# Products with v in groups of three key chunks, with a fourth exponential tile

## The chip, the cores and the metric

The kernel runs on one core of a Trainium2 chip. The metric is the device time of one execution in microseconds (us). The engines of the core are named as in the profile: PE is TensorE's matmul, PEld its weight load, DVE is VectorE, ACT is ScalarE, POOL is GpSimd and SP is SyncE, whose queue issues most DMAs.

## What is computed

One input x of 2048 tokens by 576 features goes through two branches, whose outputs are mixed by a gate per token:

```python
B, S, D = 1, 2048, 576
H = 32; Dh = D // H                    # 32 heads of 18
qkv = (x @ wqkv).reshape(B, S, 3, H, Dh)
scores = einsum("bhqd,bhkd->bhqk", q, k) * Dh ** -0.5
a = (softmax(scores) @ v) @ wo
h = gelu(layernorm(x) @ w1 + b1)       # 576 to 4608
b = h @ w2 + b2                        # 4608 to 576
g = sigmoid((x * gate_w).sum(-1))
out = g * a + (1 - g) * b
```

All of it is float32. The kernel keeps that precision with fp32r matmuls by splitting operands into a high and a low part and adding three products.

## The kernel before

**Attention.** The 32 heads form 16 pairs, and each pair is worked on in two halves of 1024 query tokens: 32 units. A unit has 16 chunks of 128 keys, so the main loop has 512 *steps* (`NSTEP`). In a step, `s2` (L268) is called twice, for two blocks of 512 queries. Each call makes the scores of both heads with two matmuls (L279), one in rows 0 to 63 of the array and one in rows 64 to 127, and ACT takes their exponentials into a tile of `RING` (L281). Between the two matmuls of `s2` stands a *round* of the maxima: two matmuls of the transposed scores (L204) whose maxima DVE reduces (L206). The rounds run about 20 steps ahead of the scores, since a unit's maxima enter its scores as two extra rows of q. They end at step 492.

**Products with v.** `pv` (L296) multiplies exponentials with v (L308): for a key chunk eight records, in four column tiles of 32, into one PSUM bank that sums a unit's 16 chunks. It is called in every even step for the two chunks before it. `RING` has three tiles: two from the pool `pp`, used at first for staging weights, and `ring2`. When a unit's sum is complete, `o_store` (L315) copies the bank with DVE and sends it off. The PSUM has three banks for the maxima (`ps_s1`), one for the sums (`ps_o`), two for scores and two for the MLP.

**MLP.** It runs in the gaps of the attention, as a generator that yields after each slot of two matmuls. It takes four token blocks, and for each nine groups of four chunks of the 4608 hidden features. A group has two *up pairs* (`h_pair`, L523: two chunks of hidden features, 27 slots that the planner counts at 231 ns, L547) and four *out pairs* (`out_pair`, L643: 128 tokens, 24 slots of 131 ns, L679). The order is up, four outs of the group before, up, so that two up pairs stand next to each other; in a block's last group the second up pair stands between the second and the third out pair. An up pair is followed by the gelu in pieces: ACT adds the bias (L572) and squares (L635), POOL multiplies (all POOL operations have line L160), ACT takes the Tanh (L628), and POOL multiplies again, rounds to `hh` and subtracts to `hl`, the two parts that the out pairs use. In the first token block the weights are split too: ACT copies (L444), POOL subtracts, and the parts go to scratch in HBM, from where the other blocks load them.

**The planner.** The order of every engine's queue is fixed when the program is built. `run_due` (L135) is called once per `s2`, per group of products and per piece of MLP; it advances a slot count and a clock `now` by the planned time, and issues what has come due: operations set for a slot (`defer`), those set for a time (`queue_end`, from `pool_end`, the planned end of POOL's work), and background work on POOL such as the split of w1, which may start when `pool_end` is less than 950 ns ahead of `now`.

**The gaps.** A step has two places, one behind each `s2`. In every two steps one place holds `pv` and three hold a *piece* of MLP, which `fill` (L1301) takes by running the generator to its next cut. Where an up pair is cut follows from `piece`, the place's number: in three pieces, or in six where the MLP is ahead of its target (`behind`) or the pair is the first of a group. An out pair is cut in three. The work is paced so that 32.6 us of MLP by the planner's count (`KEPT`) remain when the maxima end. Between two `s2` calls with nothing between them, the second waits for a bank until the exponential has read it.

**Loads of k and v.** `KA` has three tiles, taken in turn by the pairs. k, q and v of later pairs are loaded in the second step of a unit, on SP's queue.

Of the kernel before, what the change touches and what calls it, by code (L numbers as in the profile page):

```python
# [17 lines left out]
P = 128  # L18
# [36 lines left out]
BARE = NSTEP - LEAD - NT  # L55
KEPT = (FIN - BARE) / 2 * 4650.0


@with_exitstack
def gated_mix_kernel(ctx: ExitStack, tc: tile.TileContext, x, wqkv, wo, w1, b1, w2, b2, gate_w, out):  # L60
# [33 lines left out]
    ps_s1 = ctx.enter_context(tc.tile_pool(name="ps_s1", bufs=NS1, space=PSUM))  # L94
    ps_o = ctx.enter_context(tc.tile_pool(name="ps_o", bufs=1, space=PSUM))
    QA = [att.tile([P, HALF], F32R, name=f"qa{i}") for i in range(3)]
    KA = [att.tile([P, S], F32R, name=f"ka{i}") for i in range(3)]
# [81 lines left out]

    def load_k(pair, c0=0, c1=S):  # L180
        ka = KA[pair % 3]
# [11 lines left out]
    def s1_round(u, r):  # L193
# [5 lines left out]
        qa, ka = QA[u % 3], KA[UNITS[u][0] % 3]  # L199
# [38 lines left out]
    RING = []  # L238
    ybusy = [0]
# [28 lines left out]
    def s2(u, kc, qb, around, ns):  # L268

        flush()  # L270
        qa, ka = QA[u % 3], KA[UNITS[u][0] % 3]
# [4 lines left out]
        def head(h):  # L276
            ps = psum(ps_s2)
            r0 = 64 * h
            nc.tensor.matmul(ps, ka[r0:r0 + 56, kc * P:(kc + 1) * P], qa[r0:r0 + 56, qb * TB:(qb + 1) * TB],  # L279
                             start=True, stop=True)  # L280
            nc.scalar.activation(RING[n % 3][:, qb, h], ps, AF.Exp, scale=SCALE)  # L281

# [13 lines left out]
    def pv(n):  # L296

        flush()
        u, kc = divmod(n, NT)
        if kc == 0:  # L300
            OB[u] = psum(ps_o)
        v = VT[UNITS[u][0] % 2]
        for c in (n, n + 1):
            for qb in range(2):
                for h in range(2):
                    r = 32 * (2 * h + qb)
                    k = c % NT
                    nc.tensor.matmul(OB[u][r:r + 32, :], v[:, k, 19 * h:19 * h + 32], RING[c % 3][:, qb, h, :],  # L308
                                     start=(k == 0), stop=(k == NT - 1))
        if kc == NT - 2:  # L310
            o_store(u, OB.pop(u))
# [62 lines left out]
    def mlp():  # L374
# [148 lines left out]
        def h_pair(q, last, inner=False):  # L523
# [16 lines left out]
            ends = cuts(27, (5, 5, 4)[piece[0]] if last else (3, 5, 4)[piece[0]])  # L540
            if (last or spent[0] > behind[0] + AHEAD) and piece[0] == 0 and not late:

                ends = {4, 9, 14, 18, 23}
# [99 lines left out]
        def out_pair(i, t, acc):  # L643
# [12 lines left out]
            ends = {7, 15} if piece[0] == 0 else cuts(24, (3, 2, 1)[piece[0]])  # L656
# [120 lines left out]
    piece = [0]  # L777
    behind = [0.0]
# [41 lines left out]
    with ExitStack() as a:  # L820
# [205 lines left out]
        for i in range(3):  # L1026
# [82 lines left out]

    RING.append(ring2)  # L1110

# [4 lines left out]
    def out_proj():  # L1116
# [49 lines left out]
        def load_o(b, first=True, last=True):  # L1166

            if first:
                o = x_tile().rearrange("p (c n) -> p c n", c=5)
                ka, qa = {0: (KA[1], QA[2]), 1: (KA[1], QA[2]), 2: (KA[2], QA[0]), 3: (KA[1], QA[2])}[b]  # L1170
# [130 lines left out]
    def fill(step, share):  # L1301

        gap = 3 * (step // 2) + share
        t = spent[0]
        if over[0] is None and rounds:
            piece[0] = share
            behind[0] = base + (TOTAL - KEPT - base) * step / BARE
            atom()
            run_due(max(spent[0] - t, GAP))
        elif over[0] is None:  # L1310
            if not bare_at:
                bare_at.extend((gap, spent[0]))
            g0, s0 = bare_at
            stretch(s0 + (TOTAL - s0) * (gap + 1 - g0) / (1.5 * FIN - g0) - spent[0])
# [9 lines left out]
    looped[0] = True  # L1324
    for u in range(NU):
        for kc in range(NT):
            step = u * NT + kc
            if kc == 1:
                if u + 2 < NU:
                    load_q(u + 2)  # L1330
                if u % 2 == 0 and u // 2 + 1 < NPAIR - 1:
                    load_k(u // 2 + 1)
                    load_v(u // 2 + 1)
                elif u == NU - 5:
                    load_k(NPAIR - 1)
                elif u == NU - 4:
                    load_v(NPAIR - 1)
            at[0] = step

            s2(u, kc, 0, loop_round(), 462.0)  # L1340
            if kc % 2:
                fill(step, 1)
            elif step > 0:
                pv(step - 2)
                run_due(2080.0)
                if step <= 2 * LEAD:
                    next_round()
            else:
                fill(step, 2)
            s2(u, kc, 1, loop_round(), 462.0)  # L1350
            fill(step, 2 if kc % 2 else 0)
    pv(NSTEP - 2)
# [28 lines left out]
```

## Time and profile before

| | |
|---|---|
| median of 3 runs | 2254.62 us (2254.19 to 2256.15) |
| the profiled execution | 2255.1 us |
| its span | 2253.3 us |
| mean clock granted to TensorE | 0.998 |
| instructions | 51099 |
| DMA | 323.61 MB, 144 GB/s over the span |

The profile's page lists for each engine the busy time, its share of the span and the number of instructions. A group of instructions shows line, engine, operation, output and inputs, the count, busy time, the mean duration of one in ns, and the idle time before them with what ended it. A row of the timeline shows start and duration in us, line and operation, how many are merged in the row, and in brackets the idle time before it with its releaser. A row of the list of waits shows who waited for whom, the total in us, the number of times and the longest one.

Matmuls overlap in the array, so durations of single matmuls (414 ns on average for L279) add up to more than the time that passes; the starts show the pace.

### The profile page before, as it was taken

How to read it: one execution, taken by the hardware profiler on the slowest of the kernel's cores; microseconds unless marked ns; L12 is line 12 of the kernel's file. 1: busy time of each engine (PE TensorE's matmuls, PEld its weight loads, DVE VectorE, ACT ScalarE, POOL GpSimd, SP SyncE). 2: the span in 40 equal slices, each digit the busy share in tenths (PEclk: the TensorE clock that was granted, in tenths of full speed). 3: DMA queues.
4: the chain of work that ended last, by engine and by line, in shares of the span. 5: the costliest groups of instructions: out<-in, count | busy, mean ns of one | idle time of the engine just before them, and what ended most of it. 6: DMA issues, size and time to landing. Idle time of an engine off the chain costs nothing.

```text
span 2253.3 us, 51099 instructions
## 1 busy us (share of the span) xinstructions
PE 2231.5 (99%) x20569; PEld 1649.5 (73%) x20569; DVE 1671.8 (74%) x2953; ACT 1431.6 (64%) x2623; POOL 946.2 (42%) x936
## 2 busy tenths in 40 slices
PE   8999999999999999999999999999999999999999
PEld 7878766777777777777777777777777777777769
DVE  5675877777787787778777877787778777877545
ACT  4223677777776666666666666666666666666661
POOL 4002466666664444443444344434444444444420
PEclk9999999999999999999999999999999999999999
DMA  7755655545473424243264424243465233323355
GB/s 244 261 189 184 193 164 164 173 131 163 133 223 137 149 98 126 98 128 108 89 177 153 120 97 131 90 122 120 122 167 159 98 120 115 106 99 115 109 177 193
DMA packets 163218, 323.61 MB, mean 144 GB/s; under 512 B 59646, under 2 KB 86178, under 8 KB 152146
## 3 DMA queue, kind: packets, MB, share of 16 engines
q1 hardware_dynamic: 158982, 313.57, 44.0%
q10 hardware_dynamic: 4000, 6.78, 0.8%
q8 instruction: 162, 2.65, 0.5%
q14 instruction: 74, 0.61, 0.1%
HBM read 229.07 MB, written 95.16 MB: 144 GB/s over the span
## 4 chain that ended last, share of the span: by engine, by line
PE 92%; POOL 3%; DVE 2%; ACT 2%; DMA 1%; issue 0%; SPq 0%; ACTq 0%; DVEq 0%; POOLq 0%
PE ps L308 20%; PE ps L679 19%; PE ps L547 18%; PE ps L279 14%; PE ps L204 11%; PE ps L955 4%; PE ps L1263 3%; PE ps L973 2%; POOL zz L160 1%; POOL hl L160 1%; POOL w L160 1%; DVE m L206 1%; PE ps L870 0%; DMA p<-in_A_wqkv_dram 0%; ACT p L281 0%
## 5 line engine op out<-in xcount | busy, mean ns | idle before, releaser
L206 DVE TENSOR_REDUCE m<-ps 128x1 f32<-128x512 f32 x2048 | 1301.1, 684 | 299.6 <-PE ps L204 254.4
L281 ACT ACTIVATE p<-ps 128x512 f32<-128x512 f32 x1368 | 743.5, 596 | 377.5 <-PE ps L204 231.3
L279 PE MATMUL ps<-qa,ka 56*128 56x512 f32 x2048 | 715.1, 414 | 4.8 <-ACT p L281 3.8
L204 PE MATMUL ps<-ka,qa 54*128 54x512 f32 x2048 | 647.2, 418 | 3.8 <-DVE m L206 2.6
L679 PE MATMUL ps<-w,hh 64*128 64x288 f32 x4352 | 526.2, 296 | 2.4 <-ACT z L572 1.6
L279 PEld LDWEIGHTS ps<-qa,ka 56*128 56x128 f32 x2048 | 359.8, 185 | 229.6 <-issue 113.5
L547 PE MATMUL ps<-big,w 64*128 64x512 f32 x3888 | 513.9, 390 | 0.2 <-ACT vt L984 0.2
L160 POOL TENSOR_SCALAR zz<-zz 128x512 f32<-128x512 f32 x272 | 168.8, 621 | 776.5 <-ACT zz L635 693.9
L281 ACT ACTIVATE ring<-ps 128x512 f32<-128x512 f32 x680 | 369.6, 596 | 190.4 <-PE ps L204 124.9
L547 PEld LDWEIGHTS ps<-big,w 64*128 64x128 f32 x3888 | 401.6, 185 | 51.9 <-ACT vt L984 0.4
L679 PEld LDWEIGHTS ps<-w,hh 64*128 64x128 f32 x4352 | 421.7, 186 | 15.9 <-ACT z L572 2.1
L160 POOL TENSOR_TENSOR zz<-zz,z 128x512 f32<-128x512 f32 x280 | 361.4, 1291 | 34.5 <-ACT zz L637 10.5
L679 PE MATMUL ps<-w,hl 64*128 64x288 f32 x2176 | 364.8, 292 | 0.0
L204 PEld LDWEIGHTS ps<-ka,qa 54*128 54x128 f32 x2048 | 333.5, 185 | 30.0 <-DVE m L206 10.4
L308 PE MATMUL ps<-p,vt 128*32 128x512 f32 x2736 | 344.5, 598 | 0.0
L679 PEld LDWEIGHTS ps<-w,hl 64*128 64x128 f32 x2176 | 246.4, 185 | 1.4
L160 POOL TENSOR_TENSOR w<-x,w 128x576 fp32r<-128x576 f32 (+1 forms) x34 | 69.0, 2033 | 295.7 <-ACT w L444 276.5
L308 PEld LDWEIGHTS ps<-p,vt 128*32 128x32 f32 x2736 | 71.4, 109 | 153.9 <-issue 147.9
L308 PE MATMUL ps<-ring,vt 128*32 128x512 f32 x1360 | 179.1, 598 | 0.0
L160 POOL TENSOR_TENSOR hl<-zz,hh 128x512 fp32r<-128x512 f32 x134 | 172.5, 1287 | 15.2 <-ACT hh L598 4.3
L653 DVE SCALAR_TENSOR_TENSOR x<-ps,x 128x288 f32<-128x288 f32 x270 | 110.8, 452 | 83.3 <-PE ps L679 80.9
L955 PE MATMUL ps<-big,wqk 128*128 128x512 f32 x504 | 121.5, 396 | 0.4 <-ACT wqk L863 0.4
(118 smaller groups left out, 1382.8 us busy)
## 6 DMA issues: line engine op xcount, KB each, us to landing
w<-w_scr SPq DMA_DIRECT2D x54, 1152.0 KB
w<-w_scr SPq DMA_DIRECT2D x108, 576.0 KB
w_scr<-w SPq DMA_DIRECT2D x18, 1152.0 KB
w_scr<-w SPq DMA_DIRECT2D x36, 576.0 KB
qa<-qk_scr SPq DMA_DIRECT2D x192, 72.0 KB
ka<-qk_scr SPq DMA_DIRECT2D x90, 144.0 KB
x<-in_B_w_dram SPq DMA_DIRECT2D x34, 288.0 KB
qk_scr<-hh SPq DMA_DIRECT2D x36, 256.0 KB
```

Source lines behind the costliest of these rows:

```text
L160: fn(*args, **kw)
L204: nc.tensor.matmul(ps, qa[r0:r0 + 54, t * P:(t + 1) * P], ka[r0:r0 + 54, kb * TB:(kb + 1) * TB], start=True, stop=True)
L206: nc.vector.tensor_reduce(M4[u][:, h, t, kb:kb + 1], ps, axis=AX.X, op=ALU.max)
L279: nc.tensor.matmul(ps, ka[r0:r0 + 56, kc * P:(kc + 1) * P], qa[r0:r0 + 56, qb * TB:(qb + 1) * TB], start=True, stop=True)
L281: nc.scalar.activation(RING[n % 3][:, qb, h], ps, AF.Exp, scale=SCALE)
L308: nc.tensor.matmul(OB[u][r:r + 32, :], v[:, k, 19 * h:19 * h + 32], RING[c % 3][:, qb, h, :], start=(k == 0), stop=(k == NT - 1))
L547: nc.tensor.matmul(ps[h], wt[w_][r, c, :], Y[s_][r, c, :], start=(k == 0), stop=(k == 26))
L653: nc.vector.scalar_tensor_tensor(dst, ps[nn][:, :ND], 0.5, b2b[:, cs[nn]] if base else dst, op0=ALU.mult, op1=ALU.add)
L679: mm = nc.tensor.matmul(ps[nn][:, :ND], h_[r, tok], w_[p_][r, cs[nn]], start=(k == 0 or bare and k == 3 * G), stop=(k == 6 * G - 1 or bare ...
L955: nc.tensor.matmul(ps, w_[:, c, ms], big[:, s_, :], start=(k == 0), stop=(k == len(prods) - 1))
L973: nc.tensor.matmul(ps[:, :ND], big[:, s_, tok], w_[:, c, cs], start=(k == 0), stop=False)
L1263: nc.tensor.matmul(ps[t, n][:, :ND], OT[b][3][:, s_, tok], w_part(w_, c)[:, cs], start=(c == 0 and k == 0), stop=(c == 4 and k == 1))
```

## The change

A fourth tile joins `RING`. It takes the place of the third tile of `KA` (8 KB per partition each), and the third tile of `KA` comes back in its place at step 433, for the last pair alone. As long as four tiles are there (up to step 428), `pv` is called with all chunks in waiting when three wait, or when a pair of the MLP has ended and at least one waits. It may now reach from one unit into the next, so the bank of the sums is taken from a rotation that it shares with the maxima: a new sum takes the bank that is next in turn, and the old sum's bank goes to the end of the turn. `piece` counts the places since the last products, and with three chunks in waiting an up pair is cut in five pieces if it begins behind them. From step 428 on, products take two chunks again and the old cuts hold. The load of v for a later pair waits until the products that still read the tile are issued.

```diff
+NARROW = 431
...
-    ps_s1 = ctx.enter_context(tc.tile_pool(name="ps_s1", bufs=NS1, space=PSUM))
-    ps_o = ctx.enter_context(tc.tile_pool(name="ps_o", bufs=1, space=PSUM))
+    ps_x = [ctx.enter_context(tc.tile_pool(name=f"ps_x{i}", bufs=1, space=PSUM)) for i in range(NS1 + 1)]
+    turn_x = list(range(NS1))
+    held_x = [NS1]
+    class Rotating:
+        def tile(self, *args, **kw):
+            i = turn_x.pop(0)
+            turn_x.append(i)
+            return ps_x[i].tile(*args, **kw)
+    class Sums:
+        def tile(self, *args, **kw):
+            i = turn_x.pop(0)
+            turn_x.append(held_x[0])
+            held_x[0] = i
+            return ps_x[i].tile(*args, **kw)
+    ps_s1 = Rotating()
+    ps_o = Sums()
...
-    KA = [att.tile([P, S], F32R, name=f"ka{i}") for i in range(3)]
+    KA = [att.tile([P, S], F32R, name=f"ka{i}") for i in range(2)]
...
+    def k_tile(pair):
+        return KA[2 if pair == NPAIR - 1 else pair % 2]
...
+    def ring(n):
+        return RING[n % 4 if n < NARROW else (n - NARROW) % 3]
...
-    def pv(n):
+    def pv(n0, n1):
         flush()
-        u, kc = divmod(n, NT)
-        if kc == 0:
-            OB[u] = psum(ps_o)
-        v = VT[UNITS[u][0] % 2]
-        for c in (n, n + 1):
+        for c in range(n0, n1):
+            u, k = divmod(c, NT)
+            if k == 0:
+                OB[u] = psum(ps_o)
+            v = VT[UNITS[u][0] % 2]
             for qb in range(2):
                 for h in range(2):
...
-        if kc == NT - 2:
-            o_store(u, OB.pop(u))
+            if k == NT - 1:
+                o_store(u, OB.pop(u))
+        run_due(1040.0 * (n1 - n0))
...
-            ends = cuts(27, (5, 5, 4)[piece[0]] if last else (3, 5, 4)[piece[0]])
-            if (last or spent[0] > behind[0] + AHEAD) and piece[0] == 0 and not late:
-                ends = {4, 9, 14, 18, 23}
+            if room[0] == 3:
+                ends = cuts(27, max(1, 5 - piece[0]))
+            else:
+                ends = cuts(27, (5, 5, 4)[piece[0]] if last else (3, 5, 4)[piece[0]])
+                if (last or spent[0] > behind[0] + AHEAD) and piece[0] == 0 and not late:
+                    ends = {4, 9, 14, 18, 23}
...
-            ends = {7, 15} if piece[0] == 0 else cuts(24, (3, 2, 1)[piece[0]])
+            ends = {7, 15} if piece[0] == 0 else cuts(24, max(1, 3 - piece[0]))
...
-        for i in range(3):
+        for i in range(2):
             for j in range(2):
                 nc.gpsimd.memset(KA[i][64 * j + 32:64 * j + 64, :].bitcast(F32), 1.0)
...
+    ring_stack = ExitStack()
+    RING.append(ring_stack.enter_context(tc.tile_pool(name="c_ring", bufs=1, side="right")).tile([P, 2, 2, TB], F32, name="ring3"))
...
-    def fill(step, share):
-        gap = 3 * (step // 2) + share
+    ended = [0]
+    def fill(step):
         t = spent[0]
+        gap = gaps[0]
+        gaps[0] += 1
         if over[0] is None and rounds:
-            piece[0] = share
             behind[0] = base + (TOTAL - KEPT - base) * step / BARE
-            atom()
+            ended[0] = atom() == 2
+            piece[0] += 1
             run_due(max(spent[0] - t, GAP))
...
                 if u % 2 == 0 and u // 2 + 1 < NPAIR - 1:
                     load_k(u // 2 + 1)
-                    load_v(u // 2 + 1)
+                    due_v.append((u * NT, u // 2 + 1))
                 elif u == NU - 5:
+                    ring_stack.close()
+                    kp = ctx.enter_context(tc.tile_pool(name="c_ka", bufs=1, side="right"))
+                    KA.append(kp.tile([P, S], F32R, name="ka2"))
+                    for j in range(2):
+                        nc.gpsimd.memset(KA[2][64 * j + 32:64 * j + 64, :].bitcast(F32), 1.0)
                     load_k(NPAIR - 1)
                 elif u == NU - 4:
-                    load_v(NPAIR - 1)
+                    due_v.append((u * NT, NPAIR - 1))
             at[0] = step
+            room[0] = 3 if step < NARROW - 3 else 2
+            while due_v and due_v[0][0] <= done[0]:
+                load_v(due_v.pop(0)[1])
             s2(u, kc, 0, loop_round(), 462.0)
-            if kc % 2:
-                fill(step, 1)
-            elif step > 0:
-                pv(step - 2)
-                run_due(2080.0)
-                if step <= 2 * LEAD:
+            if step - done[0] >= room[0] or room[0] == 3 and ended[0] and step > done[0]:
+                pv(done[0], step)
+                done[0] = step
+                piece[0] = 0
+                ended[0] = 0
+                if extra[0]:
                     next_round()
+                    extra[0] -= 1
             else:
-                fill(step, 2)
+                fill(step)
             s2(u, kc, 1, loop_round(), 462.0)
-            fill(step, 2 if kc % 2 else 0)
-    pv(NSTEP - 2)
+            if not (room[0] == 3 and ended[0]):
+                fill(step)
+    pv(done[0], NSTEP)
```

More of the change, by code (lines that the diff above doesn't have):

```diff
@@ L178, in load_q @@
                 dma_r(nc.sync, qa[r:r + DH, :], qk_scr[part, d0:d0 + DH, half * HALF:(half + 1) * HALF])
+    def k_tile(pair):
+        return KA[2 if pair == NPAIR - 1 else pair % 2]
     def load_k(pair, c0=0, c1=S):
-        ka = KA[pair % 3]
+        ka = k_tile(pair)
         for h in range(2):
@@ L198, in s1_round @@
             M4[u] = asm.tile([P, 2, 8, 4], F32, name="m4")
-        qa, ka = QA[u % 3], KA[UNITS[u][0] % 3]
+        qa, ka = QA[u % 3], k_tile(UNITS[u][0])
         def head(h):
@@ L270, in s2 @@
         flush()
-        qa, ka = QA[u % 3], KA[UNITS[u][0] % 3]
+        qa, ka = QA[u % 3], k_tile(UNITS[u][0])
         n = u * NT + kc
@@ L280, in head @@
                              start=True, stop=True)
-            nc.scalar.activation(RING[n % 3][:, qb, h], ps, AF.Exp, scale=SCALE)
+            nc.scalar.activation(ring(n)[:, qb, h], ps, AF.Exp, scale=SCALE)
         def tail():
@@ L306, in pv @@
                     r = 32 * (2 * h + qb)
-                    k = c % NT
-                    nc.tensor.matmul(OB[u][r:r + 32, :], v[:, k, 19 * h:19 * h + 32], RING[c % 3][:, qb, h, :],
+                    nc.tensor.matmul(OB[u][r:r + 32, :], v[:, k, 19 * h:19 * h + 32], ring(c)[:, qb, h, :],
                                      start=(k == 0), stop=(k == NT - 1))
-        if kc == NT - 2:
-            o_store(u, OB.pop(u))
+            if k == NT - 1:
+                o_store(u, OB.pop(u))
+        run_due(1040.0 * (n1 - n0))
     stored = []
@@ L777, in gated_mix_kernel @@
     piece = [0]
+    room = [2]
     behind = [0.0]
@@ L1169, in load_o @@
                 o = x_tile().rearrange("p (c n) -> p c n", c=5)
-                ka, qa = {0: (KA[1], QA[2]), 1: (KA[1], QA[2]), 2: (KA[2], QA[0]), 3: (KA[1], QA[2])}[b]
+                ka, qa = {0: (KA[1], QA[2]), 1: (KA[1], QA[2]), 2: (KA[0], QA[0]), 3: (KA[1], QA[2])}[b]
                 OT[b] = [o, [ka[:, c * TB:(c + 1) * TB].bitcast(F32) for c in range(4)] + [qa[:, :TB].bitcast(F32)], ka]
@@ L1311, in fill @@
             if not bare_at:
-                bare_at.extend((gap, spent[0]))
-            g0, s0 = bare_at
-            stretch(s0 + (TOTAL - s0) * (gap + 1 - g0) / (1.5 * FIN - g0) - spent[0])
+                bare_at.extend((gap, spent[0], step))
+            g0, s0, n0 = bare_at
+            stretch(s0 + (TOTAL - s0) * (gap + 1 - g0) / (1.5 * (FIN - n0)) - spent[0])
             run_due(max(spent[0] - t, GAP))
@@ L1324, in gated_mix_kernel @@
     looped[0] = True
+    done = [0]
+    due_v = []
+    extra = [LEAD]
+    gaps = [0]
     for u in range(NU):
```

## The prediction

> **What bounds the kernel now.** I read the busy shares first, then the chain of work that ended last, then what TensorE waits for, and last the timeline of TensorE around one group of products with v.
>
> ```profile
> PE 2231.5 (99%) x20569; PEld 1649.5 (73%) x20569; DVE 1671.8 (74%) x2953; ACT 1431.6 (64%) x2623; POOL 946.2 (42%) x936
> PE 92%; POOL 3%; DVE 2%; ACT 2%; DMA 1%; issue 0%; SPq 0%; ACTq 0%; DVEq 0%; POOLq 0%
> L308 PE MATMUL ps<-p,vt 128*32 128x512 f32 x2736 | 344.5, 598 | 0.0
> L308 PE MATMUL ps<-ring,vt 128*32 128x512 f32 x1360 | 179.1, 598 | 0.0
> ```
>
> TensorE is busy for 99% and makes up 92% of the chain, so what counts is how densely its matmuls stand. The products with v (L308) are 2736 + 1360 = 4096 records, eight for a key chunk: 512 chunks, and since each call of pv takes two, 256 groups. The waits of TensorE that the profile names are small:
>
> ```profile
> PE ps L870 <- DMA x<-in_A_x_dram: 6.2, 2, 5.6
> PE ps L279 <- ACT p L281: 3.8, 7, 0.6
> PE ps L204 <- DVE m L206: 2.6, 5, 0.5
> PE ps L279 <- ACT ring L281: 1.0, 2, 0.6
> ```
>
> A switch between the 64-row form of all other matmuls of the loop and the 32-column form of the products appears in no wait. It shows in start times:
>
> ```profile
> 1006.02 0.39 PE L279 MATMUL ps<-qa,ka 56*128 56x512 f32 x1
> ...
> 1006.62 1.06 PE L308 MATMUL ps<-ring,vt 128*32 128x512 f32 x8
> 1007.50 1.04 PE L308 MATMUL ps<-p,vt 128*32 128x512 f32 x8
> 1008.47 0.49 PE L279 MATMUL ps<-qa,ka 56*128 56x512 f32 x1
> ...
> 1009.04 1.09 PE L547 MATMUL ps<-big,w 64*128 64x512 f32 x8
> 1009.97 0.39 PE L279 MATMUL ps<-qa,ka 56*128 56x512 f32 x1
> ...
> 1010.43 1.38 PE L547 MATMUL ps<-big,w 64*128 64x512 f32 x10
> ```
>
> A score round (two L279, two L204) takes 1010.43 - 1009.97 = 0.46 us. From 1006.02 to 1009.04 stand two score rounds and one group: 3.02 - 0.92 = 2.10 us for the group. Its second chunk starts 0.88 us behind the first, so two chunks are 1.76 us, and **0.34 us belong to the group as such**, whatever its size. That is the change's first prize.
>
> **The count of groups.** The order of the MLP repeats after a set of two up pairs and four out pairs. Group starts in one set:
>
> ```profile
> 996.46 1.06 PE L308 MATMUL ps<-p,vt 128*32 128x512 f32 x8
> 1013.83 1.06 PE L308 MATMUL ps<-p,vt 128*32 128x512 f32 x8
> 1020.82 1.92 PE L308 MATMUL ps<-p,vt 128*32 128x512 f32 x16
> 1028.14 1.06 PE L308 MATMUL ps<-ring,vt 128*32 128x512 f32 x8
> 1050.03 1.06 PE L308 MATMUL ps<-ring,vt 128*32 128x512 f32 x8
> ```
>
> With 1006.62 above: an up pair in three pieces takes 10.16 us in two steps, one in six pieces 7.21 + 6.99 = 14.20 us in four, and the out pairs from 1020.82 to 1050.03 take 29.21 us, 7.30 each, in two steps each. That is 53.57 us, 14 steps, seven groups. Now each up pair is cut into five pieces, which fill exactly the five places that three steps leave beside one group; an out pair keeps three pieces in two steps. Again 14 steps, but six groups. The first groups still come at steps 2, 4, 6 and 8 (out pairs of three pieces). From 8 to 428, where three chunks in waiting are given up, lie 30 sets of 14 steps: 180 groups. The last 84 steps have 42. So 4 + 180 + 42 = 226, 30 fewer: 30 x 0.34 = 10.2 us. Against it stand 30 more pieces of MLP, because a place without products is filled. The up pair in six pieces over four steps takes 14.20 - 10.16 = 4.04 us more than in three over two; four score rounds and a group are 4 x 0.46 + 2.10 = 3.94, so three more cuts cost 0.10, a cut 0.03, thirty 1.0 us. **Net: -9.2 us.** By another reading of the same rows: 14.20 us less two steps without MLP, halved (4.04 / 2 = 2.02 a step), gives 14.20 - 2.02 = 12.18 for three steps at half a group each; with a third of a group, 0.17 less: 12.0 us.
>
> The page "TensorEngine Tiling (Array Packing)" of the Trainium skill, section Key Properties, says that changing the tiling mode drains the engine, and "TensorE: Matmul & The Clock Gate", section Single matmul latency, puts a drain at about 175 ns. Two drains a group would be 0.35 us, by estimate 10.5 us for thirty; the trace's 0.34 agrees.
>
> **The waits in the first quarter.** In the first token block the MLP's weights are split on ACT and POOL, and there the out pair behind two adjacent up pairs takes longer:
>
> ```profile
> 526.64 1.06 PE L308 MATMUL ps<-ring,vt 128*32 128x512 f32 x8
> ...
> 534.12 0.50 PE L279 MATMUL ps<-qa,ka 56*128 56x512 f32 x1 [0.58 <-ACT ring L281]
> ...
> 535.03 1.06 PE L308 MATMUL ps<-p,vt 128*32 128x512 f32 x8
> ```
> ```profile
> 532.95 0.63 ACT L628 ACTIVATE zz<-zz 128x512 f32<-128x512 f32 x1 [1.43 <-POOL zz L160]
> 533.49 1.07 ACT L281 ACTIVATE ring<-ps 128x512 f32<-128x512 f32 x2
> ```
> ```profile
> 520.07 2.69 POOL L160 TENSOR_TENSOR w<-x,w 128x1152 fp32r<-128x1152 f32 x1 [1.58 <-ACT w L444]
> ```
>
> 8.39 us in place of 7.30: a Tanh (L628) stands 1.43 us in ACT's queue for POOL, the exponentials behind it come late, and TensorE's next scores wait for their banks. Of the nine waits for L281 in the list above, seven lie in seven such sets: 7 x 1.09 = 7.6 us. POOL is late because the split at 520.07 lies between the multiplies of the first up pair. The planner lets this split out only while pool_end is under 950 ahead of now. Count from the products before the first up pair: four splits of w2 (1555 each by pool_op) bring pool_end to 8761 from the first place at 2541; at the last fill now is 7623, 1138 ahead: not yet, and the square and the first multiplies come before it. With five pieces the first place is at 1848, pool_end 8068, and at the score round before the last fill now is 7392: 676 ahead, so the split goes out **before** the first up pair ends. I therefore expect most of this wait to go. But the split's copy then falls between exponentials, and the second up pair is 2.2 us shorter, so POOL has less time: bounds are all 7.6 us gained and, with the split still late, 11 us lost (per set the 1.43 us once more, now for hl; 0.61 us for two score rounds with no piece between, two exponentials of 1.07 less 0.46; as much again where the split's copy stands ahead of exponentials; less the 1.09). I take -4, nearer to the gain because the planner's sums put the split early.
>
> **Later blocks** split nothing. POOL's work for one up pair there:
>
> ```profile
> 1008.55 0.62 POOL L160 TENSOR_SCALAR zz<-zz 128x512 f32<-128x512 f32 x1 [27.36 <-ACT zz L635]
> ...
> 1010.63 0.62 POOL L160 TENSOR_SCALAR zz<-zz 128x512 f32<-128x512 f32 x1
> ...
> 1019.41 1.30 POOL L160 TENSOR_TENSOR hl<-zz,hh 128x512 fp32r<-128x512 f32 x1
> 1022.73 0.62 POOL L160 TENSOR_SCALAR zz<-zz 128x512 f32<-128x512 f32 x1 [2.03 <-ACT zz L635]
> ```
>
> 12.2 us from 1008.55 to 1020.71, then 2.03 idle. Twelve microseconds an up pair use this idle time up but need no more. Here it starts 1.93 us behind the products' start at 1006.62; products of three chunks last 0.34 + 3 x 0.88 = 2.98, so then it starts 1.05 before their end. The second up pair's first multiplies (2.1, from 1008.55 to 1010.63) are done at -1.05 + 12.2 + 2.1 = 13.2 us behind that end, and their Tanh has its turn on ACT at about 14.9: three steps, 12.0, a score round, 0.46, a piece of seven slots at the planner's 131 ns, 0.92, another round, and its two exponentials, 1.09. 1.7 us remain: I cost it at nothing, and at 1.09 us a set if that cover is gone (second rival).
>
> **The last part.** From 428 groups take two chunks again and up pairs ahead of their target six pieces, 16 steps a set. 9 up and 20 out pairs remain at 428, and six out pairs at 492, where the maxima end: 18.9 us of MLP by the planner, now 32.6.
>
> ```profile
> 2165.93 1.07 PE L308 MATMUL ps<-p,vt 128*32 128x512 f32 x8
> 2173.02 1.92 PE L308 MATMUL ps<-p,vt 128*32 128x512 f32 x16
> ```
> ```profile
> L281 ACT ACTIVATE p<-ps 128x512 f32<-128x512 f32 x1368 | 743.5, 596 | 377.5 <-PE ps L204 231.3
> ```
>
> Two steps take 7.1 us here, and with 1.95 us less MLP 5.15; their eight exponentials need 4.8 at 596 ns each. TensorE still sets the pace, barely; I charge 1 us, with bounds -3 (waits that stand there now may go) and +4.
>
> **Smaller edits.** Two memsets of KA move into step 433, unknown to the planner:
>
> ```profile
> L1028 POOL MEMSET ka<- 32x2048 f32 x6 | 10.8, 1800 | 0.2
> ```
>
> 3.6 us on POOL behind which Tanh, and SP's loads of k, may queue: +0.5, bounds 0 and 3.6. Two tiles of KA do for the loads, since the scores of the pair two before ended a step earlier, and v is loaded once its products are issued. The sums take the bank whose maximum is oldest; its reduction ended a piece of MLP earlier, and the next three banks are used before the old sums' bank returns: nothing, bounds 0 and 32 x 0.5 = 16 us.
>
> **Sum.** The profiled execution took 2255.1 us (span 2253.3), 0.5 above the median shown. -9.2 - 4 + 1 + 0.5 = -11.7: **2243 us**.
>
> **Rivals.** (1) *The first quarter eats the gain*: the split still lies behind the first up pair, and the out pair waits for hl. For it: only 274 planner units decide. 2255.1 - 9.2 + 11 is 2257; with half of the sets 2252. I take 2254. (2) *Slower*: with POOL's idle 2.03 us gone, a Tanh waits at every set as at 532.95. It decides from the point where POOL is over 1.7 us later than reckoned, for instance if squares queue behind late exponentials. 23 sets of the other blocks at 1.09 us are 25 us, the seven keep theirs: 2255.1 - 9.2 + 25 = 2271. Against it: 12.2 us of work in 12.0 leave POOL nearly even. "TensorE: Matmul & The Clock Gate" of the Trainium skill calls ACT's queue strict first-in-first-out; by that rule every such wait reaches the exponentials, as it did at 533.49. (3) *It doesn't do what it says*: stalled pairs lose step with the groups, single chunks get groups of their own, the count stays near 256: 2254. (4) *More*: all waits of the first quarter and those near the end go: 2255.1 - 9.2 - 7.6 - 3 = 2235.
>
> **Chances.** Forecast (2237 to 2249) 0.58, rival 1 0.12, rival 2 0.13, rival 3 0.08, rival 4 0.09. A measurement can tell about 0.2%, 4.5 us. Faster holds the forecast and rival 4, 0.67; within it is most of rivals 1 and 3, 0.16 of their 0.20; slower are rival 2 and the other 0.04, 0.17. The range 2234 to 2258 leaves out rival 2 and little more.
>
> **What would show it.** Groups of 24 records about 12.0 us behind the group before them, two in each set, and some 226 in all; 0.88 us between chunks. No 1.43 us before L628 in the first quarter, and the split of w1 ahead of the first multiplies. Many more waits of TensorE for L281 or L206, or POOL without idle time and ACT waiting for zz, would be rivals 1 or 2. The prediction is wrong if 0.34 us is not a group's own cost, or if pieces and groups lose step.

## The result and the profile after

The changed kernel takes 2277.19 us (median of 4 runs, 2272.95 to 2278.35) against 2254.4 before: a ratio of 1.0096, 95% interval 1.0079 to 1.0114. It is slower, where I forecast 2243 and a range up to 2258. Its profiled execution is the shortest of the four, 2272.95 us, and the numbers of the trace below are from that one.

The page of the kernel after: the busy times, the chain, the maxima (L229) and the products with v (L334).

```profile
PE 2231.5 (98%) x20569; PEld 1626.6 (72%) x20569; DVE 1678.4 (74%) x2953; ACT 1427.6 (63%) x2623; POOL 945.7 (42%) x936
PE 91%; DVE 4%; DMA 2%; ACT 1%; issue 1%; POOL 0%; ACTq 0%; SPq 0%; DVEq 0%
L229 DVE TENSOR_REDUCE m<-ps 128x1 f32<-128x512 f32 x2048 | 1302.0, 682 | 330.0 <-PE ps L227 248.7
L334 PE MATMUL ps<-p,vt 128*32 128x512 f32 x2160 | 273.9, 598 | 0.0
L334 PE MATMUL ps<-ring,vt 128*32 128x512 f32 x1936 | 248.3, 601 | 0.0
```

The same matmuls run (L334 has 2160 + 1936 = 4096 records as before), but VectorE now holds 4% of the chain in place of 2%. The list of TensorE's waits says the same:

```profile
PE ps L227 <- DVE m L229: 18.8, 25, 1.7
PE ps L306 <- ACT p L308: 3.6, 7, 1.4
PE ps L306 <- ACT ring L308: 1.2, 3, 0.4
```

The wait of a maxima round for a bank that VectorE has not yet read was 2.6 us before, five times 0.5 at most. Now it is 18.8 us, 25 times. The waits for exponentials are as they were.

**The groups do what was forecast.** TensorE's timeline in a later block, products alone; each group begins at the first row of its chunks (two rows of 8, or 16 + 8, or 8 + 16 records):

```profile
1005.16 1.07 PE L334 MATMUL ps<-p,vt 128*32 128x512 f32 x8
...
1016.28 1.06 PE L334 MATMUL ps<-ring,vt 128*32 128x512 f32 x8
1017.16 1.90 PE L334 MATMUL ps<-p,vt 128*32 128x512 f32 x16
1028.26 1.92 PE L334 MATMUL ps<-ring,vt 128*32 128x512 f32 x16
1030.00 1.04 PE L334 MATMUL ps<-p,vt 128*32 128x512 f32 x8
1036.40 1.06 PE L334 MATMUL ps<-p,vt 128*32 128x512 f32 x8
...
1045.49 1.06 PE L334 MATMUL ps<-ring,vt 128*32 128x512 f32 x8
...
1052.80 1.06 PE L334 MATMUL ps<-p,vt 128*32 128x512 f32 x8
```

Up pairs take 11.12 and 11.98 us, the out pair behind three chunks 8.14, the last one 7.31. With three undisturbed out pairs at 7.30 a set is 11.12 + 11.98 + 8.14 + 3 x 7.30 = 53.14 us, against 53.57 before. But the out pair from 1036.40 takes 9.09. In all there are 224 groups (226 forecast).

**Where the time went.** The loop runs from the first products to the start of the last group, 256.93 to 2197.70 us before and 255.79 to 2213.18 after. That is 1940.8 and 1957.4 us. 32 groups fewer at 0.334 are -10.7; so everything else in the loop costs **+27.3 us** more. The loop starts 1.1 us earlier, and 2.3 us more stand behind the last group's start: -10.7 + 27.3 - 1.1 + 2.3 = 17.8, the difference of the spans. To place the 27, I took from each interval between groups what its records need (0.334 a group, 0.88 a chunk, 0.463 a score round, 0.2315 and 0.1315 a slot of an up and of an out pair, 0.2315 a record of the last product, L1263 before and L1296 after) and summed what is left:

| steps | before | after | more |
|---|---|---|---|
| first 118 | 18.9 | 30.6 | +11.7 |
| 118 to 428 | 18.9 | 31.7 | +12.8 |
| 428 to 492 | 3.7 | 8.8 | +5.1 |
| 492 on | 2.6 | 1.3 | -1.3 |

That is +28.3; 1.0 us less of records stands in the loop after (one chunk more, eight records of the last product fewer), which leaves 27.3. An undisturbed interval leaves about 0.2 us with an out pair and 0.03 with an up pair.

**The loss in later blocks** is one event about once a unit. VectorE's timeline of the kernel after in the out pair of 9.09 us, with one row of POOL, and TensorE's row that waits for it:

```profile
1038.82 1.29 DVE L229 TENSOR_REDUCE m<-ps 128x1 f32<-128x512 f32 x2 [0.76 <-PE ps L227]
1040.06 1.29 POOL L180 TENSOR_TENSOR zz<-zz,z 128x512 f32<-128x512 f32 x1
1040.14 0.22 DVE L238 TENSOR_REDUCE nm<-m 128x16 f32<-128x64 f32 x1
1040.40 0.98 DVE L239 CAST nmh<-nm 128x16 fp32r<-128x16 f32 x1
1041.42 0.17 DVE L240 COPY nm<-nmh 128x16 f32<-128x16 f32 x1
1041.50 0.59 DVE L241 TENSOR_TENSOR nm<-nm,nmh 128x16 f32<-128x16 f32 x1
1042.01 1.27 DVE L229 TENSOR_REDUCE m<-ps 128x1 f32<-128x512 f32 x2
...
1042.74 0.50 PE L227 MATMUL ps<-ka,qa 54*128 54x512 f32 x1 [1.46 <-DVE m L229]
```

L238 to L241 are `s1_finish`: once a unit, VectorE reduces its maxima and splits them into two parts. For these 1.9 us no maximum of a new round is read, and TensorE has no bank for the next round. The same four instructions in the kernel before, and the products behind them:

```profile
1034.48 0.22 DVE L215 TENSOR_REDUCE nm<-m 128x16 f32<-128x64 f32 x1
1034.73 0.18 DVE L216 CAST nmh<-nm 128x16 fp32r<-128x16 f32 x1
1034.95 0.18 DVE L217 COPY nm<-nmh 128x16 f32<-128x16 f32 x1
1035.04 0.17 DVE L218 TENSOR_TENSOR nm<-nm,nmh 128x16 f32<-128x16 f32 x1
...
1035.45 1.07 PE L308 MATMUL ps<-p,vt 128*32 128x512 f32 x8
```

There a group begins at once, and its 2.1 us need no bank of the maxima: VectorE catches up for nothing. In the program's order a finish is issued at step 12 of each unit, and before, with groups on every even step, a group stood right behind it in 31 of 31 units. In the kernel after it does so in 7. The sums above agree: in steps 118 to 492 the 24 intervals in which a finish falls hold 16.1 us more than undisturbed ones would (-0.1 before), all other intervals together 1.6 us (-0.5 before).

**The first quarter** shows the mishap that I had called rival 1. POOL's timeline, TensorE's slots of the out pair, the groups around them and two rows of VectorE:

```profile
412.04 2.69 POOL L180 TENSOR_TENSOR w<-x,w 128x1152 fp32r<-128x1152 f32 x1 [1.89 <-ACT w L471]
...
416.67 1.92 PE L334 MATMUL ps<-p,vt 128*32 128x512 f32 x16
...
421.27 0.22 DVE L238 TENSOR_REDUCE nm<-m 128x16 f32<-128x64 f32 x1
421.50 1.28 POOL L180 TENSOR_TENSOR hl<-zz,hh 128x512 fp32r<-128x512 f32 x1
421.53 1.28 DVE L239 CAST nmh<-nm 128x16 fp32r<-128x16 f32 x1
421.57 0.32 PE L709 MATMUL ps<-w,hl 64*128 64x288 f32 x2
421.96 0.50 PE L306 MATMUL ps<-qa,ka 56*128 56x512 f32 x1
...
424.17 0.50 PE L227 MATMUL ps<-ka,qa 54*128 54x512 f32 x1 [1.71 <-DVE m L229]
...
429.72 1.06 PE L334 MATMUL ps<-ring,vt 128*32 128x512 f32 x8
```

The split of w1 (412.04) lies among the first up pair's multiplies. The second `hl` is written only from 421.50 on, the planner's order stops the out pair after two slots of its second piece, and a place is left empty. The pair takes three steps instead of two, 13.05 us from 416.67 to 429.72. Here a finish (421.27) falls into the same pair, and the wait of 1.71 us at 424.17 is TensorE's wait for that.

Five out pairs are stopped in this way. Three of them hold no finish and take 10.88 to 10.89 us, and each leaves 1.8 us more than an undisturbed pair: that is the price of the stop itself, 9.0 us for five. The +11.7 of the first 118 steps are then: 9.0 for the stops; 2.4 for the five up pairs ahead of them, 0.5 each; 5.9 for four finishes, two in stopped pairs and two in the out pairs from 547.10 and 605.91; 1.7 for a stretch of low clock (last section); less 6.7 for six waits for a Tanh that are gone, and 0.6 less elsewhere. The stops are also what moves the groups: each adds a step, and five of them turn the later groups of two chunks from even to odd steps, away from the finishes. From step 118 to 492 such groups stand on odd steps in 117 of 121 cases.

### The profile page after: what moved, and what is told of

Same layout as the page of the kernel before. It is cut to its first block, busy times and chain, and to the rows that moved or that the text cites. A ratio compares the mean times of both kernels' runs of the same rounds, so it can differ in the third digit from the quotient of the medians.

```text
span 2271.1 us, 51135 instructions
## 1 busy us (share of the span) xinstructions
PE 2231.5 (98%) x20569; PEld 1626.6 (72%) x20569; DVE 1678.4 (74%) x2953; ACT 1427.6 (63%) x2623; POOL 945.7 (42%) x936
## 4 chain that ended last, share of the span: by engine, by line
PE 91%; DVE 4%; DMA 2%; ACT 1%; issue 1%; POOL 0%; ACTq 0%; SPq 0%; DVEq 0%
PE ps L334 20%; PE ps L577 19%; PE ps L709 19%; PE ps L306 13%; PE ps L227 11%; PE ps L986 4%; DVE m L229 2%; PE ps L1004 2%; PE ps L1296 1%; PE ps L901 1%; DMA qa<-mr 0%; DMA dn_scr<-dn 0%; DVE nmh L239 0%; DMA big<-y_scr 0%; PE ps L1035 0%
## 5 line engine op out<-in xcount | busy, mean ns | idle before, releaser
L229 DVE TENSOR_REDUCE m<-ps 128x1 f32<-128x512 f32 x2048 | 1302.0, 682 | 330.0 <-PE ps L227 248.7
L308 ACT ACTIVATE p<-ps 128x512 f32<-128x512 f32 x1080 | 587.1, 596 | 332.4 <-PE ps L227 172.0
L308 ACT ACTIVATE ring<-ps 128x512 f32<-128x512 f32 x968 | 526.0, 596 | 273.6 <-PE ps L227 162.0
L227 PE MATMUL ps<-ka,qa 54*128 54x512 f32 x2048 | 649.5, 416 | 20.2 <-DVE m L229 18.8
L577 PEld LDWEIGHTS ps<-big,w 64*128 64x128 f32 x3888 | 388.8, 185 | 67.5 <-ACT vt L1015 0.4
L709 PE MATMUL ps<-w,hl 64*128 64x288 f32 x2176 | 371.8, 292 | 0.0
L334 PE MATMUL ps<-p,vt 128*32 128x512 f32 x2160 | 273.9, 598 | 0.0
L709 PEld LDWEIGHTS ps<-w,hl 64*128 64x128 f32 x2176 | 252.2, 185 | 1.4
L334 PE MATMUL ps<-ring,vt 128*32 128x512 f32 x1936 | 248.3, 601 | 0.0
L334 PEld LDWEIGHTS ps<-p,vt 128*32 128x32 f32 x2160 | 58.1, 109 | 128.1 <-issue 121.0
L334 PEld LDWEIGHTS ps<-ring,vt 128*32 128x32 f32 x1936 | 52.3, 109 | 116.0 <-issue 115.7
```

What stands on the lines that cost most here:

```text
L227: nc.tensor.matmul(ps, qa[r0:r0 + 54, t * P:(t + 1) * P], ka[r0:r0 + 54, kb * TB:(kb + 1) * TB], start=True, stop=True)
L229: nc.vector.tensor_reduce(M4[u][:, h, t, kb:kb + 1], ps, axis=AX.X, op=ALU.max)
L308: nc.scalar.activation(ring(n)[:, qb, h], ps, AF.Exp, scale=SCALE)
L577: nc.tensor.matmul(ps[h], wt[w_][r, c, :], Y[s_][r, c, :], start=(k == 0), stop=(k == 26))
L709: mm = nc.tensor.matmul(ps[nn][:, :ND], h_[r, tok], w_[p_][r, cs[nn]], start=(k == 0 or bare and k == 3 * G), stop=(k == 6 * G - 1 or bare ...
```

## The experiments

Theory A: the finish of the maxima lost its place ahead of the products. Theory D: the late `hl` in the first quarter. Rivals: B, sharing the banks costs; C, groups of three starve VectorE or ScalarE wherever they stand. "Finishes in place" is the number of units, of 31, in which a group stands right behind the finish in the program's order. The traces agree within two (a group begins within 2.2 us of the finish in 31 units before, 6 after, 25 in e3, 18 in e5 and 5 in e6), except in e1 and e4.

| run | built on | groups | finishes in place | median us | ratio to before, 95% |
|---|---|---|---|---|---|
| e1_finish | after | 224 | 31 | 2283.77 | 1.013 (1.0115 to 1.0145) |
| e2_away | before | 256 | 0 | 2264.22 | 1.0036 (1.0022 to 1.0051) |
| e3_first | after | 234 | 25 | 2254.75 | 1.0001 (0.9992 to 1.001) |
| e4_three | e1, e3 | 234 | 31 | 2275.13 | 1.009 (1.0075 to 1.0105) |
| e5_phase | after | 224 | 20 | 2266.01 | 1.0051 (1.0037 to 1.0065) |
| e6_first_phase | e3 | 234 | 4 | 2270.51 | 1.0072 (1.0058 to 1.0085) |
| e7_split | after | 226 | 24 | 2259.34 | 1.0021 (1.0012 to 1.003) |
| e8_before_split | before | 256 | 31 | 2257.01 | 1.001 (1.0001 to 1.002) |
| e9_hl | after | 226 | 24 | 2259.86 | 1.0018 (1.0009 to 1.0027) |
| e10_hl_split | e9 | 226 | 24 | 2254.51 | 1.0002 (0.9993 to 1.0011) |
| e11_hl_step12 | e9 | 228 | 28 | 2251.99 | 0.9989 (0.998 to 0.9998) |
| e12_all | e10, e11 | 228 | 28 | 2248.74 | 0.9974 (0.9963 to 0.9984) |

**e1_finish** puts each finish right ahead of the next products, wherever these are.

```diff
+        while finish:
+            s1_finish(finish.pop(0))
...
-            defer(1, lambda: s1_finish(u))
+            if looped[0]:
+                finish.append(u)
+            else:
+                defer(1, lambda: s1_finish(u))
```

> The changed kernel, with the finish of a unit's maxima (nm, its cast, copies and transpose on DVE) issued right ahead of the next products, where 31 of 31 finishes of the kernel before stand within 2.2 us ahead of a group, and not one slot behind the last round. Theory A, that the finish now falls into out pairs and makes TensorE wait for DVE: the waits of L227 for DVE fall from 18.8 us to under 7, and of the 2277 us about 18 go: 2256 to 2262. Rival B, that the bank shared by sums and maxima makes TensorE wait for DVE: the waits stay at 15 us or more and the time within 4 us of 2277. Rival C, that groups of three starve ACT and DVE: no change either.

It missed: 2283.77 us. The waits of TensorE show that the edit did one thing and broke another:

```profile
PE ps L306 <- DMA qa<-mr: 14.5, 9, 3.5
...
PE ps L227 <- DVE m L229: 5.9, 12, 1.3
```

The wait for VectorE fell from 18.8 to 5.9 us, but where the next group is steps away the finish now comes so late that the rows of maxima reach q behind the scores that need them. It can't decide on A; it shows that the finish may not be moved back freely. Nor does the finish stand ahead of the group on the chip: VectorE still has the round before it to reduce, and in 30 of 31 units the finish starts 1.2 to 1.6 us behind the start of the group, so within it.

**e2_away** issues the finish three slots later, behind the products, in the kernel before, where nothing else is changed.

```diff
-            defer(1, lambda: s1_finish(u))
+            defer(4 if looped[0] else 1, lambda: s1_finish(u))
```

> The kernel before with one number changed: the finish of the maxima three slots later, so that it falls behind the products, among the pieces of MLP. Theory A: with a finish in out pairs in some 17 of 31 units at 0.7 to 1.5 us each, 12 to 25 us slower than before: 2267 to 2280, with waits of L204 for DVE over 10 us. Rivals B and C, for which the place of the finish doesn't matter: 2254 within 3 us.

2264.22 us: 9.5 us slower than the 2254.7 beside it, and below the 2267 to 2280 expected. The wait for VectorE rose from 2.6 to 5.9 us and not over 10. The trace shows why the sign is weak: the finish starts 0.3 to 1.6 us behind the start of a group in every unit, so it is still partly covered by the group's 2.1 us and not among the pieces of MLP. Two things more are in this trace and not in that of before, a wait of 2.3 us for a load from `w_scr` (L679) and a granted clock of 0.57 and 0.61 in the windows 494 to 498 and 1689 to 1693. So the place has a price in a kernel without groups of three, but this run does not give it cleanly.

**e3_first** keeps groups of two in the first 118 steps.

```diff
-            room[0] = 3 if step < NARROW - 3 else 2
+            room[0] = 3 if 118 <= step < NARROW - 3 else 2
```

> The changed kernel, with groups of two and the old cuts for the first 118 steps (the first token block, where weights are split) and groups of three only from there. Theory D, that the out pair behind two adjacent up pairs now waits there, since POOL's split of w1 still lies inside the first up pair's multiplies and both up pairs are over 2.2 us sooner: the first 470 us of the loop lose about 12 us of waits and gain 2 us of groups, so 2265 to 2270. If the first block is not to blame: 2277 to 2281.

It was expected at 2265 to 2270 and came at 2254.75, 22 us under the kernel after, with shared banks throughout and groups of three in 310 of 512 steps. That speaks against B and C. It also showed what I had not seen when I wrote the expectation: without the stopped out pairs the groups of two chunks stay on even steps (4 of 121 from step 118 to 492 are on odd ones), so that 25 finishes are in place. The edit repairs the later blocks too. The 7.3 us that 22 groups fewer should save do not show in the time.

```profile
PE ps L227 <- DVE m L229: 3.8, 8, 0.6
```

**e4_three** joins e1, e3 and groups at even steps from 428 on.

```diff
-            if step - done[0] >= room[0] or room[0] == 3 and ended[0] and step > done[0]:
+            if step - done[0] >= room[0] and (step < NARROW - 3 or step % 2 == 0) or room[0] == 3 and ended[0] and step > done[0]:
```

> The changed kernel with the finish ahead of products, groups of two in the first 118 steps, and in the last 84 steps groups at even steps alone, so that no group of one chunk is left at the end. If A and D are the whole loss, what remains is the saving of about 23 groups at 0.33 us: 7 us faster than before, 2244 to 2250. If something else costs (B or C), 2255 or more.

2275.13 us, a miss by e1's fault: its rows of maxima are late for 10.3 us in seven waits. It says nothing beyond e1.

**e5_phase and e6_first_phase** test A with one and the same edit on two kernels. Two more rounds of maxima at the start put every finish one step earlier. On the kernel after that brings 20 finishes into place instead of 7; on e3 it leaves 4 of 25.

```diff
-    extra = [LEAD]
+    extra = [LEAD + 2]
```

> The changed kernel with the maxima two rounds, one step, further ahead (six extra rounds in place of four). The groups stay where they are. A unit's finish then falls one step earlier: counted in the program, 20 of 31 finishes stand right ahead of a group instead of 7. Theory A (a finish away from a group makes TensorE wait for DVE): 13 waits of about 1 us go and two rounds cost 1 us more at the start: 2262 to 2267, L227 waiting for DVE under 9 us. If only the length of groups or the shared bank counted: 2277 to 2280.

> The kernel with groups of two in the first 118 steps, which took 2254.8, with the same two rounds more. Its finishes, 25 of 31 right ahead of a group, become 4 of 31. Theory A: 21 waits come: 2266 to 2278, L227 waiting for DVE over 10 us. Otherwise 2255 to 2258.

Both times came as A had it: 11.2 us **less** than the kernel after (2266.01 against 2277.19) and 15.8 us **more** than e3 (2270.51 against 2254.75). The wait for VectorE in e5, which was expected under 9 us and missed that, then in e6:

```profile
PE ps L227 <- DVE m L229: 11.7, 19, 1.7
```
```profile
PE ps L227 <- DVE m L229: 15.9, 25, 1.7
```

In e5 what the intervals of steps 118 to 492 hold beyond their records is 27.3 us, against 40.5 in the kernel after and 22.6 before; the first 118 steps, with the five stopped pairs still there, are at 33.3. In steps 118 to 492 the 24 intervals with a finish hold 4.0 us more than undisturbed ones, where the kernel after had 16.1. No theory in which the extra rounds, the banks or the size of the groups cost by themselves gives opposite signs. Nor does the length of the finish's cast (last section): the 31 casts of the loop take 16.7 us in e5 and 13.6 in the kernel after, 11.3 in e6 and 11.4 in e3. A is shown.

**e7_split and e8_before_split** hold w1's split back until POOL has been idle for 600 ns of the planner's time, in the kernel after and before.

```diff
-            queue = raw[0] ** 2 * SLOT
+            queue = 4 * SLOT if raw[0] == 2 else -600.0 if looped[0] else SLOT
```

> The changed kernel, where the planner may start the split of w1 only when POOL has had nothing to do for 600 ns, so that it falls behind the multiplies of both up pairs. Counted in the program: 226 groups, no out pair over three steps, all of two-chunk groups at even steps and 24 of 31 finishes right ahead of a group. Theory D (the split in the middle of the first up pair's multiplies stops the out pair, and the step that it adds turns the groups from even to odd steps): both losses go, 2241 to 2249, and the first block is faster than before by 4 us or more. If the split's place doesn't matter: 2270 or more.

> The kernel before with the same rule for the split of w1, groups as they were. The seven Tanh waits of the first block, 1.09 us each, go: 2247 to 2249. If they have another cause, 2254.

Both missed in the total. e7 gains 18 us on the kernel after: no out pair takes three steps, 24 finishes are in place. But once, in the up pair from 388.99, the split comes so late that the up pair forces it while its load is still under way. ACT waits 7.7 us for that load, and the exponentials behind it hold up TensorE:

```profile
PE ps L306 <- ACT p L308: 9.2, 6, 6.4
```

In e8 the same happens (5.05 us of TensorE ahead of 401.52), and it eats what is gained: five of the seven waits for a Tanh, 1.1 us each, are gone with the split's place, as the prediction had named their cause. The first and the last stay (the out pairs from 307.93 and 674.10 take 8.39 and 8.47 us). The median is 2257.01 all the same; ten runs lie between 2255.33 and 2258.55, one at 4318.33.

**e9_hl** changes one number of the kernel after: the planner takes `hl` as ready 500 ns earlier.

```diff
-                    queue_end(-1000.0, update)
+                    queue_end(-1500.0, update)
```

> The kernel after, with one number changed: the planner takes the lower half of a pair's activations as ready 1500 ns ahead of the end it reckons for GpSimd, not 1000. The out pair behind the late split of w1 then no longer stops in the planner's order, so no out pair of the first block takes a third step, the groups stay on even steps, 226 groups stand in place of 224, and 24 of the 31 finishes of the maxima stand right ahead of a group instead of 7. Theory (place of the finish, and the stop that moves the groups): the residual returns to about that of the kernel before plus 2 to 4, the groups' saving of about 10 stays: 2244 to 2252 us, and about 6 us of waits of TensorE on VectorE's maxima or less. Rival (the stop was right: TensorE now waits on the chip for the lower half, 1 to 2 us in each of the seven first quarters' out pairs, and its clock falls): 2256 to 2266 us, with waits of the products of h on GpSimd. Rival (the groups of three cost by themselves): 2268 us or more.

2259.86 us, 17.3 us under the kernel after, yet above the 2244 to 2252 expected and inside the 2256 to 2266 of the first rival. Groups around the place shown above, a finish in a later block with its group, and the waits, all of e9:

```profile
414.05 1.06 PE L334 MATMUL ps<-ring,vt 128*32 128x512 f32 x8
...
423.28 1.92 PE L334 MATMUL ps<-ring,vt 128*32 128x512 f32 x16
```
```profile
1038.20 0.17 DVE L239 CAST nmh<-nm 128x16 fp32r<-128x16 f32 x1
...
1038.91 1.92 PE L334 MATMUL ps<-ring,vt 128*32 128x512 f32 x16
```
```profile
PE ps L227 <- DVE m L229: 4.1, 9, 0.7
PE ps L709 <- POOL hl L180: 3.9, 5, 0.8
```

The out pair now takes 9.23 us in two steps, not 13.05 in three, and the finish stands ahead of a group again. The rival's waits for `hl` are there too, five of 0.8 us at most where it had seven of 1 to 2. Seven of the eleven runs, those with a granted clock of 0.996 to 0.998, took 2258.79 to 2260.92, and four with 0.999 or 1.0 took 2255.0 to 2255.73; this goes with some 5 us of the miss. Even the four are 3 us above the range.

**e10_hl_split and e11_hl_step12** add to e9, the first an earlier split of w1, the second a group at the step of the finish.

```diff
-            queue = raw[0] ** 2 * SLOT
+            queue = 4 * SLOT if raw[0] == 2 else 2400.0
```
```diff
-            if step - done[0] >= room[0] or room[0] == 3 and ended[0] and step > done[0]:
+            if step - done[0] >= room[0] or room[0] == 3 and ended[0] and step > done[0] or step % NT == NT - 4 and step > done[0] + 1:
```

> As the run before it (1500 ns), and the split of w1 may be issued while GpSimd still has up to 2400 ns to do, not 950, so it is issued ahead of the first up pair's end where the planner asks for it. Theory: same 226 groups and 24 of 31 finishes; the split's copy on ScalarE then stands ahead of the Tanh waits instead of among them, worth between +3 and -6 against the run before it: 2240 to 2254 us. Rival: the split's GpSimd part stands ahead of the first up pair's own multiplies and the chain ends as late as in the kernel after: waits on the chip, 2256 us or more.

> As the first run of this call (1500 ns), and a group is also issued at a unit's step 12, where the finish of its maxima is issued, if two or more chunks are due: 228 groups, 28 of 31 finishes ahead of a group. Theory (place of the finish): two groups more cost 0.7, four finishes more in place give back 0.7 to 1.7 each: 3 us less to 2 us more than the first run of this call, 2241 to 2252 us. Rival (the place of the finish does not matter by itself and the parity does, since some groups now stand on odd steps again): 2256 us or more.

2254.51 us is half a microsecond beyond what was expected of e10; 2251.99 is at the upper edge of that of e11. That is 7.9 us under e9's median, but not the worth of two groups and four finishes alone. In e11 no run has a clock under 0.998, and against the four runs of e9 with 0.999 or 1.0 it is 3.0 to 3.7 us. In the profiled executions, too, a wait of 2.3 us for a load from `w_scr` in e9 is not in e11, and the steps from 492 on hold 8.8 us beyond their records in e9 and 3.1 in e11.

**e12_all** is e10 and e11 together.

> The last two runs put together: lower half taken as ready 1500 ns ahead, a group also at a unit's step 12, and the split of w1 issued with up to 2400 ns left on GpSimd. 228 groups, 28 of 31 finishes in place. Theory: the residuals of the two add up. In the first block the waits of the products of h for the lower half (five times 0.6 to 0.8, 3.8 in all) and the six or so waits of about 0.8 for the Tanh go, as they went with the earlier split: 5 to 8 us less than 2252, so 2243 to 2249 us, 0.2 to 0.5 per cent under the kernel before. Rival (the earlier split moves w1's loads and stores onto the loads of y, as the one interval of 4.8 us too much behind 1165 showed, and the clock falls there): 2250 to 2254 us.

2248.74 us, within the theory's range: 28.5 us under the kernel after and 0.26% under the kernel before (0.16 to 0.37%). Its out pair at the shown place, and its waits:

```profile
417.74 1.06 PE L334 MATMUL ps<-ring,vt 128*32 128x512 f32 x8
...
425.90 1.92 PE L334 MATMUL ps<-ring,vt 128*32 128x512 f32 x16
```
```profile
PE ps L227 <- DVE m L229: 3.5, 7, 0.6
PE ps L1043 <- DVE big L1045: 1.8, 1, 1.8
...
PE ps L709 <- POOL hl L180: 0.8, 1, 0.8
```

8.16 us, as an out pair behind three chunks takes without a wait. Its loop is 1930.5 us, 10.3 under that of the kernel before: 28 groups fewer are -9.35, eight records of the last product that stand behind the loop -1.85, and what the intervals hold beyond their records +0.9: -4.3 in the first 118 steps, where the earlier split also removes most of the waits for a Tanh of the kernel before, +4.6 from 118 to 428, where four intervals at added groups hold 1.3 us each with a wait for ScalarE, and +0.6 behind. So the groups' saving is there once groups and finishes stand right. 4.1 us are lost again ahead of the loop (3.1) and behind it (1.0). The first goes with the earlier split, whose limit also holds ahead of the loop: e10 and e12 alone start the loop at 259.85 and 260.03 us (e9 at 255.68, e11 at 257.47) and alone have the wait of L1043. The kernel before was not run with the earlier split, so how much of the 0.26% belongs to the change is not parted.

## Why the prediction was wrong

**The count and the price of a group: right.** 224 groups came for 226, a set shrank by 53.57 - 53.14 = 0.43 us against the 0.34 less one cut of 0.03 that I had. In e12 the loop is 10.3 us shorter, near the 9.2 that the sum began with; there the groups are 9.4 of it, and gains and losses of other kinds nearly cancel.

**The first quarter: the step that failed is "676 ahead, so the split goes out before the first up pair ends".** I compared the planner's sums and not the moment at which the generator asks for that split. It asks at the start of the second up pair (`prep` in `pair`), so the limit of 950 was met, but the request came in the middle of the first pair's multiplies. The term of -4 was +11.7 on the trace. The number is near my bound of 11 lost, but its parts are not mine: the stops and the up pairs ahead of them, less the waits for a Tanh, are 9.0 + 2.4 - 6.7 = 4.7 us, and the finishes, which the bound did not hold, are 5.9. Rival 1 had the stop, but took it to end near 2254, since it did not see what the stopped pairs (five, where I had counted seven sets) do to all later groups.

**The later blocks: the step that failed is "I cost it at nothing".** I followed POOL and ScalarE there, and rightly: no Tanh waits as rival 2 had it. But the sum has no term for the finish of the maxima at all; VectorE enters it only with the bank of the sums, at "nothing, bounds 0 and 32 x 0.5 = 16 us". The row of 2.6 us for its waits seemed to say that it had room; it was small because once a unit a group of products stood behind the finish and hid it. The change moves the groups, and that cover is gone. The rows needed were in the trace of before: 1034.48 to 1035.45 is shown above. This cost most of the +12.8 us up to step 428: 10.9 us beyond undisturbed intervals in the 20 intervals with a finish, against -0.2 before.

**The last part: +1 forecast, +5.1 - 1.3 found.** From 428 to 492 groups stand on odd steps, the same fault; e5 brings these steps from 8.8 to 4.1 us, near the 3.7 of before. The memset, +0.5, shows in no wait.

**Rival 2's time, 2271, was nearest**, but not its cause: the slower end came from VectorE's queue, not from POOL's and ScalarE's. Rival 3 (the count stays near 256) did not happen. My range ended at 2258 because it left rival 2 out and priced each rival alone, and because one stopped pair was not asked what it does to the order behind it.

**What stays open.** No run takes the sharing of the banks away by itself; e12, which shares them throughout, holds 0.9 us more beyond its records than the kernel before, so its price is small, but it isn't measured. Why some runs wait for a load from `w_scr` is not shown. Nor is it settled how much of the last 4 to 5 us between the runs of one kernel is the clock below.

## What to carry to other kernels

When work is regrouped, list for every engine what its burst instructions (a finish once a unit) were hidden behind, and look in the new order whether that cover still stands at the same place: a short row in the list of waits can mean good cover, not spare room. A piece that slips by one step in a periodic order shifts everything behind it against everything with another period, so a local stall has to be priced for the whole rest. Ask when a planner is asked for an operation, not only when its limit allows it.

## What the hardware showed

**Behind short waits the clock can fall, and need not.** The kernel after, windows of 4 us; the fields are window, its length, busy time of PE, PEld, DVE, ACT and POOL, then the granted clock:

```profile
484.00:488.00 4.00, 2.70 (x24) 1.70 (x20) 3.97 (x10) 3.63 (x7) 2.21 (x4) 1.00 0.01 5
488.00:492.00 4.00, 4.00 (x24) 1.01 (x24) 1.44 (x3) 1.40 (x3) 3.92 (x3) 0.57 0.02 3
...
1040.00:1044.00 4.00, 2.54 (x31) 2.19 (x29) 3.90 (x10) 1.35 (x3) 3.19 (x3) 1.00 0.00 0
1044.00:1048.00 4.00, 4.00 (x41) 2.10 (x39) 2.67 (x6) 2.02 (x5) 0.00 (x0) 1.00 0.02 3
```

In the first window TensorE was busy for 2.70 of 4 us, with two waits for VectorE of 0.38 and 0.92 us, and was granted 0.57 in the next 4. The group of three chunks there took 4.41 us to the next scores (488.12 to 492.53), against 2.71 for the one at 416.67: 1.3 us of waits cost 1.7 more. In the third window TensorE was busy for less, 2.54 us, with a wait of 1.46, and the clock stayed at 1.00. So the length of the waits alone does not decide, and these runs do not show what does. "TensorE: Matmul & The Clock Gate" of the Trainium skill, section Part 1: The HAM clock gate, puts the fall behind an idle window of about 3.4 us; here no such window stood, and the row decides. The clock goes with the difference between runs of one kernel: the three other runs of the kernel after had 0.996 to 0.997 and took 2276.7 to 2278.4 us, the profiled one 0.999 and 2272.95.

**A small cast on VectorE can take seven times as long.** L239 casts 16 values a partition. It takes 0.17 to 0.18 us in most units of the kernel before and in about half of those after, but 0.98 at 1040.40 above, where it ended just as a multiply of POOL did (1040.06 with 1.29 us), and 1.28 at 421.53, where POOL's subtraction from 421.50 ended with it. "SBUF — State Buffer" of the Trainium skill, section Who interferes with whom, says that a cast on VectorE can need the port pair that it shares with GpSimd, and then waits for the whole of GpSimd's instruction; the rows agree. 15 of 31 casts took over 0.3 us after and 5 before, 13.6 and 9.0 us in all, so this can be only the smaller part of the loss.
